# Feed-forward products in two column halves, in an attention and ReGLU kernel with a stored order

## The chip, the cores and the metric

The kernel runs on one core of a Trainium2 chip. The metric is the device time of one execution in microseconds. Before the change it was 398.09 us, the median of three runs (398.03, 398.09 and 399.47). A difference counts as faster or slower in this document when it exceeds 0.5% of that, about 2 us.

The core has a matrix engine (PE, with its weight loads shown apart as PEld), three engines for element work (DVE, ACT and POOL), and a queue of DMA issues that SyncE (SP) works off. Each engine takes its own instructions in the order in which the program lists them and waits at an instruction until what that one needs is there.

## The reference

Attention over 8 sequences of 576 rows with 8 heads of 64, each with 16 beacon rows in front that every query sees, and then a feed-forward layer over all 4608 rows:

```python
k_all = np.concatenate([beacon_k, k], axis=2)          # (8, 8, 592, 64)
v_all = np.concatenate([beacon_v, v], axis=2)
scores = scale * np.matmul(q, k_all.transpose(0, 1, 3, 2))
scores = np.where(causal, -1000000000.0, scores)       # the beacons are never masked
a = np.exp(scores - scores.max(-1, keepdims=True))
a /= a.sum(-1, keepdims=True) + 1e-09
attn_out = np.matmul(a, v_all)
x = attn_out.transpose(0, 2, 1, 3).reshape(4608, 512)
gate = np.maximum(x @ w_gate, 0.0)                      # 512 -> 1536
val = x @ w_val
out = gate * val @ w_out                                # 1536 -> 512
```

## The kernel before

**Attention.** A sequence is taken in two quads of two head pairs each. Score products (L828) use the array as four quarters of 64 rows by 64 columns; the last 16 query rows of all heads of a sequence go together through L878 with four strips of 32 columns. DVE adds the mask and takes the row's extreme (L776), ACT takes the exponential with the row's sum (L783), DVE the reciprocal (L789), and POOL multiplies with it (L794), which gives the tile `pb` (for the last rows `pa`). A transposing DMA on SP's queue (L914) turns `pb` into `pTb`, for the first sequence PE does it (L904). The value products (L924) then use the array as two halves of 128 rows by 64 columns, one head of the pair in each:

```python
def product(d0, w, c, last, rows, rhs):
    for hh in range(2):
        h = 2 * p + hh
        nc.tensor.matmul(ps.tile[64 * hh:64 * hh + 64, d0:d0 + w], t.v.tile[:rows, c, D * h:D * h + D],
                         rhs(64 * hh), start=(c == 0), stop=(c == last))
```

Their result goes from PSUM to `xT`, the transposed input of the feed-forward layer. Queries, keys and values come by DMA into staging tiles `st`, are rounded to bf16 tiles `h` (L546, L501, mostly on POOL) and turned (L557 and L630 on PE, L602 by DMA for the last sequence).

**Feed-forward.** The 4608 rows are cut into ten spans of 240 to 512 rows. For each of the twelve 128-column blocks of a span there is a `gate` task (L985) and a `val` task (L990), each of four matmuls with 128 by 128 weights over up to 512 columns, ACT takes the ReLU (L996), DVE multiplies (L1001) into `hT`. Twelve output products (L1016) for every 128 rows follow, in three `outp` tasks of four matmuls. All of these use the array whole, except the last 64 rows of all: there each matmul has 64 weight columns and the two halves of the array take the two halves of the output.

**Order.** Every piece is a task with an engine, and the text `ORDER` lists all tasks in the order in which they are written into the program. An entry is a task's number, a letter for the engine where there is a choice, and the tiles or PSUM banks it takes; `f4:7` is a filler, four matmuls on a zero tile (L1068), which stands where PE would otherwise idle. There are eight PSUM banks, and a product that takes a bank waits until the bank's former content is read. Since the order is fixed, an instruction at the head of an engine holds up all behind it.

I call a change from one way of dividing the array to another a switch of form. The forms are whole (L557, L904, L947, L985, L990, L1016, fillers), halves (L924), quarters (L828, L630) and strips (L878).

## Time and profile before

| | |
|---|---|
| Median of three runs | 398.09 us |
| Profiled execution | 397.86 us, span 396.1 us |
| PE busy | 382.1 us (96% of the span) |
| DVE, ACT, POOL busy | 280.1, 268.1, 231.4 us |
| Granted PE clock | 0.998 |

The span runs from the first to the last instruction; the rest of the profiled time lies around it. A busy PE is not a PE at its peak: a matmul row shows its whole passage, 379 ns for 512 columns, while the next one starts some 216 ns after it. What counts is therefore the distance between starts. In the views by line, "idle before" is the time the engine stood before an instruction and the name behind the arrow is what ended it; "issue" means that the profile shows nothing that it waited for. Attention ends near 333 us; after that PE does feed-forward products alone.

### The profile page before, as it was taken

What the parts mean: (1) busy time and instruction counts of PE and PEld (TensorE: products, weight loads), DVE (VectorE), ACT (ScalarE), POOL (GpSimd) and SP (SyncE); (2) the same over time, 40 slices, a digit from 0 to 9 for tenths busy, and PEclk for the clock granted to TensorE, in tenths of its full rate; (3) what the DMA queues carried; (4) which work ended last, traced back from release to release, by engine and by line L of the source; (5) the groups of instructions that cost most, each with busy time, mean ns of one, the idle gap of its engine ahead of it and who ended that gap; (6) DMA issues with size and microseconds to landing.
All of it is one profiled execution on the core that took longest, in us unless ns stands there. A gap on an engine that the chain in (4) does not pass through costs nothing.

```text
span 396.1 us, 10057 instructions
## 1 busy us (share of the span) xinstructions
PE 382.1 (96%) x3416; PEld 202.2 (51%) x3461; DVE 280.1 (71%) x1018; ACT 268.1 (68%) x832; POOL 231.4 (58%) x448
## 2 busy tenths in 40 slices
PE   6799999999999999999999999999999999999996
PEld 4568856654554445454444454544454544444443
DVE  5998899979967898878777885687847831431531
ACT  3999799897887787778775978587847723231121
POOL 3899779949695778495856766663891550000000
PEclk9999999999999999999999999999999999999999
DMA  7999999999999999989999899899889274000202
GB/s 188 231 228 225 212 223 214 206 214 214 242 187 224 268 205 201 202 225 169 223 208 229 181 211 191 182 191 185 153 165 201 52 130 117 26 0 2 107 29 93
DMA packets 184100, 68.89 MB, mean 174 GB/s; under 512 B 158384, under 2 KB 179504, under 8 KB 184048
## 3 DMA queue, kind: packets, MB, share of 16 engines
q1 hardware_dynamic: 179216, 63.46, 75.3%
q0 software_dynamic: 4752, 4.72, 7.3%
q8 instruction: 27, 0.44, 0.5%
q14 instruction: 25, 0.20, 0.2%
q10 hardware_dynamic: 80, 0.07, 0.1%
HBM read 38.54 MB, written 9.44 MB: 121 GB/s over the span
## 4 chain that ended last, share of the span: by engine, by line
PE 79%; DMA 7%; POOL 4%; DVE 3%; issue 3%; ACT 2%; SPq 1%; POOLq 0%; ACTq 0%; DVEq 0%
PE f L990 21%; PE f L985 21%; PE f L1016 20%; PE f L924 6%; PE f L828 5%; DMA pTb<-pb 4%; POOL pb L794 3%; PE f L557 2%; PE f L904 1%; POOL h L546 1%; DMA st<-in_q_dram 1%; ACT pb L783 1%; DVE f L776 1%; DMA st<-in_k_dram 1%; PE f L947 1%
## 5 line engine op out<-in xcount | busy, mean ns | idle before, releaser
L794 POOL TENSOR_SCALAR pb<-pb,small 128x256 bf16<-128x256 bf16 (+8 forms) x272 | 143.1, 546 | 53.8 <-DVE small L789 50.4
L783 ACT ACTIVATE pb<-f,small 128x320 bf16<-128x320 f32 (+8 forms) x272 | 144.3, 545 | 28.6 <-DVE small L776 19.3
L776 DVE CUSTOM_DVE_ANT_0 f<-f,mask 128x64 f32<-128x64 f32 (+8 forms) x288 | 136.2, 508 | 18.0 <-PE f L828 10.4
L985 PE MATMUL f<-xT,wg_r 128*128 128x512 bf16 (+3 forms) x468 | 107.7, 357 | 0.7
L990 PE MATMUL f<-xT,wv_r 128*128 128x512 bf16 (+3 forms) x464 | 106.0, 357 | 1.3 <-issue 0.5
L1001 DVE TENSOR_TENSOR hT<-g,f 128x512 bf16<-128x512 f32 (+3 forms) x120 | 73.8, 628 | 41.9 <-PE f L990 30.4
L1016 PE MATMUL f<-wo_r,hT 128*128 128x512 bf16 (+3 forms) x439 | 99.8, 374 | 1.7 <-issue 0.8
L996 ACT ACTIVATE g<-f 128x512 f32<-128x512 f32 (+3 forms) x120 | 65.1, 562 | 46.8 <-PE f L985 41.4
L990 PEld LDWEIGHTS <-wv_r 128*128 128x128 bf16 x480 | 44.6, 98 | 44.9 <-issue 3.5
L985 PEld LDWEIGHTS <-wg_r 128*128 128x128 bf16 x480 | 44.9, 98 | 43.7 <-issue 2.3
L1016 PEld LDWEIGHTS <-hT 128*128 128x128 bf16 (+3 forms) x456 | 42.0, 100 | 46.8 <-issue 2.3
L546 POOL TENSOR_SCALAR h<-st 128x512 bf16<-128x512 f32 (+1 forms) x88 | 47.8, 555 | 22.5 <-DMA st<-in_q_dram 4.9
L783 ACT ACTIVATION_READ_ACCUMULATOR pb<-f,small 128x1 f32 x272 | 58.1, 214 | 0.0
L776 DVE DVE_READ_ACCUMULATOR2_ANT small<- 128x1 f32 x296 | 41.5, 140 | 0.0
L828 PE MATMUL f<-kT,qT 64*64 64x64 bf16 (+7 forms) x640 | 34.0, 292 | 1.0 <-ACT kT L497 0.8
L499 DVE COPY osb<-f 128x512 f32<-128x512 f32 (+3 forms) x22 | 14.8, 674 | 22.6 <-PE f L1016 22.5
L497 ACT CAST xT<-f 128x240 bf16<-128x240 f32 (+2 forms) x39 | 14.9, 388 | 23.0 <-PE f L924 20.8
L924 PE MATMUL f<-pTb,v 128*64 128x320 bf16 (+3 forms) x488 | 27.3, 254 | 0.8 <-DMA pTb<-pb 0.7
L501 POOL TENSOR_SCALAR v<-st 128x512 bf16<-128x512 f32 (+1 forms) x38 | 23.6, 625 | 7.1 <-DMA st<-in_v_dram 6.9
L789 DVE RECIPROCAL small<-small 128x1 f32<-128x1 f32 (+3 forms) x136 | 19.8, 160 | 10.0 <-ACT pb L783 8.5
L924 PEld LDWEIGHTS <-v 128*64 128x64 bf16 (+1 forms) x512 | 21.3, 109 | 10.0 <-issue 5.7
L828 PEld LDWEIGHTS <-qT 64*64 64x64 bf16 x640 | 14.5, 105 | 22.5 <-issue 17.8
(64 smaller groups left out, 229.1 us busy)
## 6 DMA issues: line engine op xcount, KB each, us to landing
out_dram<-osb SPq DMA_DIRECT2D x34, 256.0 KB, 3.0
st<-in_k_dram SPq DMA_DIRECT2D x28, 256.0 KB, 4.5
st<-in_q_dram SPq DMA_DIRECT2D x28, 256.0 KB, 4.1
st<-in_v_dram SPq DMA_DIRECT2D x24, 256.0 KB, 4.9
st<-in_q_dram SPq DMA_DIRECT2D x16, 128.0 KB, 3.4
st<-in_k_dram SPq DMA_DIRECT2D x16, 128.0 KB, 3.1
st<-in_v_dram SPq DMA_DIRECT2D x8, 224.0 KB, 4.5
wv_r<-in_moe_w_val_dram POOLq DMA_DIRECT2D x3, 512.0 KB, 7.6
```

Source lines behind the costliest of these rows:

```text
L501: nc.gpsimd.tensor_scalar(dst, src, 1.0, 1.0, ALU.mult, ALU.mult)
L546: (nc.gpsimd if x.engine == "POOL" else nc.vector).tensor_scalar(to, src, by, 1.0, ALU.mult, ALU.mult)
L776: nc.vector.tensor_tensor_reduce(out=view(i, n - m), in0=view(i, n - m), in1=msk, scale=1.0, scalar=at(7) if m < n else 3.0e38, op0=ALU.ad ...
L783: nc.scalar.activation(ph.tile.rearrange("p a n -> p (a n)")[:, a:a + n], view(i), AF.Exp, bias=at(i), scale=-1.0, accum_out=at(4 + i))
L794: nc.gpsimd.tensor_scalar(one, one, at(8 + i), 1.0, ALU.mult, ALU.mult)
L828: nc.tensor.matmul(banks[k][b_].tile[64 * i:64 * i + 64, off:off + n], t.q.tile[r, 2 * g + i, 64 * j:64 * j + 64], t.kT.tile[r, 2 * g + i, ...
L924: nc.tensor.matmul(ps.tile[64 * hh:64 * hh + 64, d0:d0 + w], t.v.tile[:rows, c, D * h:D * h + D], rhs(64 * hh), start=(c == 0), stop=(c == ...
L985: nc.tensor.matmul(psg.tile[:, :mt], wg_r[:, ki, nf * P:(nf + 1) * P], xT[:, ki, m0:m0 + mt], start=(ki == 0), stop=(ki == KM - 1))
L990: nc.tensor.matmul(psv.tile[:, :mt], wv_r[:, ki, nf * P:(nf + 1) * P], xT[:, ki, m0:m0 + mt], start=(ki == 0), stop=(ki == KM - 1))
L996: r = add("ACT", c_act(mt), lambda _, psg=psg, g=g: nc.scalar.activation(g.tile[:, :mt], psg.tile[:, :mt], AF.Relu), (a,), (psg, g), -1000 ...
L1001: hid.append(add("DVE", c_dve(mt), lambda _, psv=psv, g=g, nf=nf: nc.vector.tensor_mul(hT[nf].tile[:, :mt], g.tile[:, :mt], psv.tile[:, :m ...
L1016: nc.tensor.matmul(ps[c].tile[64 * c:64 * c + rows, :w], hT[nf].tile[:, t0:t0 + rows], wo_r[:, nf, w * c:w * c + w], start=(nf == 0), stop ...
```

## The change

A task can be marked `w` in the stored order. A marked `gate`, `val` or `outp` task issues every matmul twice, for columns 0 to 63 and for columns 64 to 127 of its weights, each with its own weight load, into the upper and lower half of the same bank. This is the array form of the value products. The moving operand and the number of moving columns stay the same, so a pair does the work of one matmul. The order is a new one as well. The diff, cut to its core:

```diff
 ORDER = """
 ...
-394:0 1619 1620 1521 1613 2181 1601 1621 2174:3 1616 1565:0 1622 1627:6.7.4.5 403 1561:0 1623 1636 1563:2 1602 1562a 1628 1605 2182 400:2 1629 2185:0
 ...
+1621 1601 2174:3 1620 2181 1602 1612 1604 1619 1565:0 2176 1611 1622 1627:6.7.4.5 1561:0 1623 1563:2 1562v 2177w 1635 2185w:0 1636 1629 395 1638 2182w
 ...
@@ class Task
         self.start = None
+        self.narrow = False
@@ replay
-            t = self.tasks[int(what.rstrip("avg"))]
-            t.engine = engines.get(what[-1], t.engines[0])
+            t = self.tasks[int(what.rstrip("avgw"))]
+            t.engine, t.narrow = engines.get(what[-1], t.engines[0]), what[-1] == "w"
@@ kernel
+    def halves(x):
+
+        return ((0, 64), (64, 64)) if x.narrow else ((0, P),)
@@ ffn
-            def gate(_, nf=nf, psg=psg):
+            def gate(x, nf=nf, psg=psg):
                 for ki in range(KM):
-                    nc.tensor.matmul(psg.tile[:, :mt], wg_r[:, ki, nf * P:(nf + 1) * P], xT[:, ki, m0:m0 + mt],
-                                     start=(ki == 0), stop=(ki == KM - 1))
+                    for c, w in halves(x):
+                        nc.tensor.matmul(psg.tile[c:c + w, :mt], wg_r[:, ki, nf * P + c:nf * P + c + w], xT[:, ki, m0:m0 + mt],
+                                         start=(ki == 0), stop=(ki == KM - 1))
 ...
                     for nf in range(k * part, k * part + k):
-                        for c in range(halves):
+                        if groups == 1 and rows == P:
+                            for c, z in halves(x):
+                                nc.tensor.matmul(ps[0].tile[c:c + z, :w], hT[nf].tile[:, t0 + c:t0 + c + z],
+                                                 wo_r[:, nf, :w], start=(nf == 0), stop=(nf == NF - 1))
+                            continue
+                        for c in range(groups):
```

`val` is changed as `gate` is. The turning of rounded tiles (L557) could be marked too, but no such task is. Marked are 23 tasks: one `gate` of the first span (240 columns) and, from the fifth span on, 13 `outp`, 5 `gate` and 4 `val` tasks with 512 columns. With four matmuls each these are 92 pairs in place of 92 matmuls. The fillers shrink from 79 to 76 matmuls.

The new order is close to the old one. Of PE's 599 entries 109 stand elsewhere among their neighbours, mostly by one or two places. POOL and SP are reordered more, and five copies out of PSUM go from DVE to ACT.

The first place is PE's order at the value products of the seventh sequence's second quad, near 288 to 297 us. In the rows `v` and `hT` behind LDWEIGHTS are weights (values and hidden tiles), and the first number of a shape is the number of output rows. Before, the value products are followed by seven `outp` tasks, more value products, four feed-forward tasks and the strip scores:

```order
L924 MATMUL f<-pTb_80,v_87 64x64
L1016 LDWEIGHTS hT_106
L1016 MATMUL f<-wo_r,hT_106 128x512
...
L1016 MATMUL f<-wo_r,hT_121 128x512
L924 LDWEIGHTS v_87
L924 MATMUL f<-pTb_79,v_87 64x320
...
L924 MATMUL f<-pTb_79,v_87 64x128
L1016 LDWEIGHTS hT_106
L1016 MATMUL f<-wo_r,hT_106 128x512
...
L985 MATMUL f<-xT,wg_r 128x512
L878 LDWEIGHTS qT_84
```

After, with the same tasks but for one `outp` that has gone behind the second value products:

```order
L929 MATMUL f<-pTb_80,v_87 64x64
L1024 LDWEIGHTS hT_106
L1024 MATMUL f<-wo_r,hT_106 64x512
...
L1024 MATMUL f<-wo_r,hT_121 64x512
L929 LDWEIGHTS v_87
L929 MATMUL f<-pTb_79,v_87 64x320
...
L929 MATMUL f<-pTb_79,v_87 64x128
L1024 LDWEIGHTS hT_106
L1024 MATMUL f<-wo_r,hT_106 64x512
...
L991 MATMUL f<-xT,wg_r 64x512
L883 LDWEIGHTS qT_84
```

The form changed at four borders here (values to `outp`, `outp` to values, values to `outp`, `gate` to strips); now it changes at one, the last.

Counted along the whole of PE's order, the form changes 177 times before and 174 times after. In PE's first 50 entries, up to about 30 us of the trace before, the number rises from 24 to 27; behind them it falls from 153 to 147. The six fewer lie at four groups of marked tasks: one near 206 us, one near 254 us, three at the place shown, one near 308 to 313 us.

The second place is SP's queue near 257 to 272 us, in front of the transposition `pTb_80<-pb_74`, whose result the value products at 271.56 us read. Before:

```order
L914 DMA_TRANSPOSE pTb_81<-pb_73 128x25x128
L914 DMA_TRANSPOSE pTa_77<-pa_71 128x5x128
L588 DMA st_95<-in_k_dram 128x4x64 x2
L914 DMA_TRANSPOSE pTb_80<-pb_74 128x25x128
L602 DMA_TRANSPOSE qT_84<-h_101 128x4x128
```

After:

```order
L919 DMA_TRANSPOSE pTb_81<-pb_73 128x25x128
L1042 DMA out_dram<-osb_97 128x512
L919 DMA_TRANSPOSE pTb_80<-pb_74 128x25x128
L919 DMA_TRANSPOSE pTa_77<-pa_71 128x5x128
L607 DMA_TRANSPOSE kT_86<-h_100 128x4x128
```

The small transposition now stands behind it, the loads of `st_95` further ahead, and one store of the output has come between.

The third place is POOL's order there. The last two rows with `pb_74` are what that transposition waits for; `h` rows are rounded inputs, `v` rows rounded values. Before:

```order
L794 TENSOR_SCALAR pa_71<-pa_71,small 128x592
L794 TENSOR_SCALAR pb_74<-pb_74,small 128x384
L501 TENSOR_SCALAR v_88<-st_89 128x512
L794 TENSOR_SCALAR pb_74<-pb_74,small 128x448
L794 TENSOR_SCALAR pb_74<-pb_74,small 128x320
L546 TENSOR_SCALAR h_100<-st_91 128x512
L794 TENSOR_SCALAR pb_74<-pb_74,small 128x128
L794 TENSOR_SCALAR pb_74<-pb_74,small 128x576
L794 TENSOR_SCALAR pb_74<-pb_74,small 128x256
L546 TENSOR_SCALAR h_102<-st_92 128x512
```

After:

```order
L506 TENSOR_SCALAR v_88<-st_89 128x512
L799 TENSOR_SCALAR pb_73<-pb_73,small 128x384
L799 TENSOR_SCALAR pb_73<-pb_73,small 128x576
L799 TENSOR_SCALAR pb_74<-pb_74,small 128x128
L799 TENSOR_SCALAR pb_74<-pb_74,small 128x448
L799 TENSOR_SCALAR pa_71<-pa_71,small 128x592
L799 TENSOR_SCALAR pb_74<-pb_74,small 128x320
L551 TENSOR_SCALAR h_100<-st_91 128x512
L551 TENSOR_SCALAR h_102<-st_92 128x512
L799 TENSOR_SCALAR pb_74<-pb_74,small 128x576
L799 TENSOR_SCALAR pb_74<-pb_74,small 128x256
```

Three pieces of `pb_74` and the values' rounding have moved ahead of the row with `pa_71`, and the rounding of `st_92` has moved from behind the last two pieces to ahead of them. On DVE the reciprocal that these two need stands ahead of one feed-forward product (L1001) that it stood behind.

## The prediction

> I read the page first, then PE by stretches of time, PE's rows at the marked tasks, and last the engines behind the one long wait that PE has.

> **What bounds the kernel.** The page's span, its busy times and its slices:

> ```profile
> span 396.1 us, 10057 instructions
> PE 382.1 (96%) x3416; PEld 202.2 (51%) x3461; DVE 280.1 (71%) x1018; ACT 268.1 (68%) x832; POOL 231.4 (58%) x448
> PE   6799999999999999999999999999999999999996
> POOL 3899779949695778495856766663891550000000
> PEclk9999999999999999999999999999999999999999
> ```

> PE is busy in every slice, and its clock is never held back. By three stretches (microseconds from the start; length, PE busy, matmuls):

> ```profile
> 0.00:30.00 30.00, 24.23 (x260) 1.00 1.06 216
> 30.00:271.50 241.50, 237.82 (x2396) 1.00 1.01 209
> 271.50:392.30 120.80, 119.91 (x763) 1.00 0.44 95
> ```

> So after 30 us PE stands idle for 3.7 and 0.9 us, and the end moves with PE: with how long its matmuls take, how often the form changes, and with the few waits. That also caps the gain. The change removes no arithmetic.

> **The pair itself.** A marked task issues two half-width matmuls in place of one, so 92 pairs. The price of a pair against one whole matmul decides all else. The trace has the same form in the last 64 rows of the output and in the value products; here beside the whole form, PE's rows and then the loads:

> ```profile
> L1016 PE MATMUL f<-wo_r,hT 128*128 128x512 bf16 x391 | 92.3, 379 | 1.7 <-issue 0.8 <-ACT g L996 0.3
> L1016 PE MATMUL f<-wo_r,hT 128*64 128x256 bf16 x24 | 1.5, 275 | 0.0
> L1016 PEld LDWEIGHTS <-hT 128*128 128x128 bf16 x408 | 38.1, 98 | 44.9 <-issue 1.9
> L924 PEld LDWEIGHTS <-v 128*64 128x64 bf16 x448 | 18.1, 109 | 9.3 <-issue 5.7 <-DMA pTb<-pb 1.1
> L1016 PEld LDWEIGHTS <-hT 128*64 128x64 bf16 x24 | 1.2, 110 | 0.4 <-issue 0.4
> ```

> The 24 half matmuls are 12 pairs in 1.5 us. Less the last one's passage of 0.275 us, 11 distances of 0.11 us are left for 256 columns. Four whole matmuls of 512 columns take 1.03 us (rows of L985 below), which less 0.379 us leaves three distances of 0.217 us, twice that. So both halves stream at once, at full rate. Their loads are slow for their width, 110 ns for 64 columns against 98 ns for 128, but 24 of them fit in 1.2 us, one pair of loads in 0.1 us: the two run beside each other and under the matmuls. I cost the 92 pairs at nothing. [...] Upwards the bound is a pair whose two loads run in turn, 0.220 against 0.217 us, together +0.3 us. Below nothing there is no room, since the columns streamed are the same.

> [...]

> **Switches of form.** PE around the first place shown of the order (start, length, then the group):

> ```profile
> 287.74 0.88 PE L924 MATMUL f<-pTb,v 128*64 128x128 bf16 x16
> 288.55 6.22 PE L1016 MATMUL f<-wo_r,hT 128*128 128x512 bf16 x27
> 294.70 0.88 PE L924 MATMUL f<-pTb,v 128*64 128x320 bf16 x16
> 295.51 1.04 PE L1016 MATMUL f<-wo_r,hT 128*128 128x512 bf16 x4
> 296.39 1.03 PE L985 MATMUL f<-xT,wg_r 128*128 128x512 bf16 x4
> ```

> The seven `outp` tasks end at 294.77; their last matmul therefore starts at 294.77 - 0.379 = 294.39, and a next one of the same form would start at 294.61. The value products start at 294.70. A switch costs 0.09 to 0.10 us, and I take 0.10. Behind the first 30 us the order has six fewer (153 to 147): -0.6 us. Each is saved only if PE has its next work ready, so the bounds are -0.6 and 0. The three more in the first 30 us stand among fillers and waits (below), so I cost them at nothing, at most +0.3.

> **The wait at 271.56.** Two of the six lie ahead of this place, so I ask what they meet there. PE, then SP's queue, and the step of the chain of waits between them:

> ```profile
> 270.02 0.88 PE L924 MATMUL f<-pTb,v 128*64 128x320 bf16 x16
> 271.56 0.88 PE L924 MATMUL f<-pTb,v 128*64 128x128 bf16 x16 [0.66 <-DMA pTb<-pb]
> ```
> ```profile
> 257.23 4.21 SPq L914 DMA_TRANSPOSE pTb<-pb  x1
> 261.54 1.22 SPq L914 DMA_TRANSPOSE pTa<-pa  x1
> 262.81 1.12 SPq L588 DMA_DIRECT2D st<-in_k_dram  x2
> 264.03 4.28 SPq L914 DMA_TRANSPOSE pTb<-pb  x1
> ```
> ```profile
> 264.03 7.48 DMA pTb<-pb
> ```

> It is the one wait of PE after 30 us of more than a few tenths, and it ends when a transposition lands 7.48 us after its issue at 264.03. Whatever PE gains before it is lost unless this issue comes earlier. The queue is released of 1.22 + 1.12 us ahead of it and gets one store (some 0.5 us), so SP would be free near 262.0 instead of 263.9. The other condition is POOL and, ahead of it, DVE:

> ```profile
> 258.07 0.76 POOL L794 TENSOR_SCALAR pa<-pa,small 128x592 bf16<-128x592 bf16 x1 [2.50 <-DVE small L789]
> 261.06 0.62 POOL L546 TENSOR_SCALAR h<-st 128x512 bf16<-128x512 f32 x1
> 261.65 1.69 POOL L794 TENSOR_SCALAR pb<-pb,small 128x128 bf16<-128x128 bf16 x3
> 263.31 1.21 POOL L546 TENSOR_SCALAR h<-st 128x512 bf16<-128x512 f32 x2
> 261.28 0.69 DVE L1001 TENSOR_TENSOR hT<-g,f 128x512 bf16<-128x512 f32 x1 [0.17 <-ACT pb L783]
> 261.88 0.16 DVE L789 RECIPROCAL small<-small 128x2 f32<-128x2 f32 x1
> ```

> POOL idles 2.50 us at `pa`, while other rows behind it stand ready. The new order puts three `pb_74` rows and a value rounding in front of `pa`, and pays with one more rounding (0.6 us) ahead of the last two. The reciprocal for these two, at 261.88, now goes before a product of 0.69 us. So the two can start near 261.3 and end near 262.6, and the transposition issues some 1.4 us earlier, or 0.7 if the reciprocal stays late. PE gets there 0.2 us earlier, so 0.86 us are wanted. I take the wait as gone: -0.66; bounds -0.66 and, if nothing moves, +0.2 (the two switches eaten). The small transposition, pushed behind, is issued some 5 us later than now; its readers come after 273 us and it takes under 3 us (the row of all transpositions below has 2.6 as the least), so I cost it at nothing, with perhaps 1 us of cover left.

> **What else moves.** 109 PE entries, the five copies given to ACT, and many POOL and SP rows are reordered. In the trace before, PE had 3.7 + 0.9 us of idle time after 30 us, the wait just counted among it, so the new waits can cost more than the old ones can give back. I take +0.2 us; bounds -0.5 and +3 (next part). At the start:

> ```profile
> L1068 PE MATMUL f<-idle 128*128 128x256 bf16 x79 | 12.8, 302 | 2.3 <-DVE idle L442 2.0
> 12.52 1.16 PE L1068 MATMUL f<-idle 128*128 128x256 bf16 x9
> 14.85 0.62 PE L557 MATMUL f<-ident,h 128*128 128x128 bf16 x8 [1.17 <-DVE small L789]
> ```

> Fillers and waits for other engines fill this stretch. Three fillers less take nothing off the path, and a score group moved behind a turning fits in waits like that of 1.17 us; 0, with 0.5 us either way.

> **Sum.** 0 - 0.6 - 0.66 + 0.2 + 0 = -1.06 us. The profiled execution took 397.86 us and becomes 396.8; it lies 0.23 us under the median of the runs, so I give 397.0 us for the median. That is -0.3%, within the 0.5% which this measurement can tell from no change.

> **Rivals.** *The savings are eaten.* If the transposition lands at 271.5 as now, PE waits longer and only the four switches behind count: 398.09 - 0.4 = 397.7. For it: a reciprocal that depends on rows reordered on ACT and DVE. Against it: the freed SP queue.

> *POOL stalls in front of a transposition.* POOL takes its rows in order and stood 2.50 us at 258.07 and longer still here:

> ```profile
> 248.80 0.43 POOL L794 TENSOR_SCALAR pb<-pb,small 128x192 bf16<-128x192 bf16 x1 [3.14 <-DVE small L789]
> L914 SPq DMA_TRANSPOSE pTb<-pb x28: 3679/4188/5597, 63.1 to 323.4; - x28
> DMA to landing us min/median/max: 2.6/6.2/8.6
> ```

> The new order could put such a stall ahead of one of the 28 transpositions whose landing PE just meets, as at 271.56. PE then stands for the stall less what cover there is: 3.14 us on top of -0.6 gives 398.09 + 2.5 = 400.6. It decides the sign from 0.6 us on, and makes the kernel slower by over 0.5% from 2.6 us on. For it: most of POOL's rows moved. Against it: at the place I could follow, the move takes a stall away.

> *The start gives more.* If the first stretch loses 1 us of its waits, the forecast of 397.0 becomes 396.0. For it: 12.8 us of fillers and the waits among them. Against it: they end on DMAs and element work, which the marks don't touch.

> *The halves don't overlap.* A load of 110 ns shown by each of 92 pairs is +10.1 us, with the forecast 407. [...]

> **Chances.** Forecast 0.43 (396.2 to 397.6), eaten 0.20, POOL's stall 0.25, a better start 0.09, no overlap 0.03. Under 396.1 lie the better start and the lower edge of the forecast, 0.12. Over 400.1 lie 0.17 of the stall, the last rival and a little for several small new waits, 0.21. The rest, 0.67, is within 0.5%. The range 395.8 to 400.6 leaves out the last rival and the ends of the second and third.

> **What would show it.** PE's rows with half the columns: 512-column pairs 0.217 us apart. At 288 to 297 us one group of half form with no load idling in it. The value products near 271 us without a wait for the DMA, their transposition issued near 262.6 us. PE's busy share unchanged. The forecast is wrong if pairs lie further apart, or if a wait of over 1 us for a transposition or for PSUM appears on PE.

## The result and the profile after

| | before | after |
|---|---|---|
| Median, first series (20 runs each) | 398.71 us | 397.46 us |
| Ratio, 95% interval | | 0.9965 (0.9949 to 0.9981) |
| Median, second series (28 and 12 runs) | 398.32 us | 397.80 us |
| Ratio, 95% interval | | 0.9975 (0.9956 to 0.9994) |
| Profiled execution, span | 397.86, 396.1 us | 398.12, 396.4 us |

The changed kernel is 0.25 to 0.35% faster. That is less than the 0.5% taken as a difference, but both intervals lie below 1. The forecast was 397.0 us. One of the 20 runs of the changed kernel took 557.51 us at a clock of 0.66, and one of the 23 runs of the kernel before in the first series of experiments 1356.71 us at full clock; the ratios leave both out.

The page of the profile after, and PE by the three stretches used before (length, PE busy, matmuls, granted clock, DMA share, GB/s):

```profile
span 396.4 us, 10292 instructions
PE 386.1 (97%) x3550; PEld 205.3 (52%) x3550; DVE 279.2 (70%) x1013; ACT 269.2 (68%) x837; POOL 232.3 (59%) x448
PEclk9899999999999999999999999999999999999999
```
```profile
0.00:30.00 30.00, 24.37 (x245) 0.94 1.05 199
30.00:271.50 241.50, 240.52 (x2439) 1.00 1.00 211
271.50:392.30 120.80, 120.80 (x868) 1.00 0.42 97
```

Three things stand out. This execution is longer than the profiled one of before although the median is lower. The clock was not full in the first 30 us. And PE seems to have gained 3.6 us of busy time behind 30 us, far more than the forecast takes off. Most of the last one is an artefact. The page of before counts 3416 matmuls beside 3461 weight loads; this page counts 3550 of both. Where the record of a matmul is missing, the trace shows idle time that was none: 0.05 us for one out of a stream of 512 columns (two distances of 0.216 us less one passage of 0.379 us), up to 0.16 us elsewhere.

PE after at the two places of the prediction (start, length, group):

```profile
271.37 0.55 PE L833 MATMUL f<-kT,qT 64*64 64x512 bf16 x12
271.85 1.57 PE L929 MATMUL f<-pTb,v 128*64 128x320 bf16 x32
...
288.73 0.88 PE L929 MATMUL f<-pTb,v 128*64 128x128 bf16 x16
289.44 5.35 PE L1024 MATMUL f<-wo_r,hT 128*64 128x512 bf16 x48
294.62 0.86 PE L929 MATMUL f<-pTb,v 128*64 128x320 bf16 x16
295.31 1.89 PE L1024 MATMUL f<-wo_r,hT 128*64 128x512 bf16 x16
297.04 1.03 PE L991 MATMUL f<-xT,wg_r 128*64 128x512 bf16 x8
```

The value products run as one group of 32 without a wait. At 289 to 298 us the half form goes through: eight matmuls of `gate`, four pairs, take 1.03 us, as four whole ones did. The six `outp` tasks end at 294.79, their last pair started at 294.79 - 0.379 = 294.41, and the value products follow 0.21 us behind it, the distance within a form.

**Where the time went.** The tasks are the same in both kernels, so I took the start of a task's first weight load in each trace and subtracted that of before. Only tasks are shown that stand at comparable places in both orders. Positive is later, in us; the heads are the times in the trace of before. The rows below the first two are the experiments of the next section.

| kernel | 26.2 | 37.2 | 62.6 | 101.8 | 270.0 | 271.6 | 287.7 | 299.1 | 316.4 | 390.9 |
|---|---|---|---|---|---|---|---|---|---|---|
| after | 1.53 | 1.63 | 2.42 | 2.38 | 1.83 | 0.96 | 0.99 | 0.65 | 0.40 | 0.28 |
| after, second profile | 1.49 | 1.58 | 1.67 | 1.63 | 1.07 | 0.20 | 0.22 | -0.11 | -0.37 | -0.49 |
| new order, no marks | 0.47 | 0.57 | 0.82 | 0.78 | 0.48 | -0.40 | -0.37 | -0.37 | -0.53 | -0.65 |
| old order, marks | 0.65 | 0.64 | 0.64 | 0.67 | 1.53 | 0.66 | 0.69 | 0.36 | 0.25 | 0.24 |
| old order, queue freed | 1.42 | 1.42 | 1.42 | 1.42 | 1.62 | 0.93 | 0.93 | 0.93 | 0.93 | 0.93 |
| new start, old rest | 0.84 | 0.94 | 1.04 | 1.18 | 1.21 | 0.98 | 0.98 | 0.98 | 0.98 | 0.67 |
| old start, new rest | 1.57 | 1.57 | 1.57 | 1.39 | 0.83 | -0.04 | -0.01 | -0.34 | -0.61 | -0.73 |
| the same, second profile | -0.14 | -0.14 | -0.14 | -0.32 | -0.88 | -1.76 | -1.73 | -2.06 | -2.33 | -2.45 |

The changed kernel loses 1.5 us at the start and regains 2.15 us behind 62.6 us, alike in both of its profiles: 0.6 up to the wait near 271.6 us, 0.87 there and some 0.7 behind it. At 57.8 us its first profile alone has a wait of 0.57 us for a weight's DMA.

Part of the loss at the start belongs to no kernel. PE by windows of 3 us, of before and then of the changed kernel (behind the comma PE busy, matmuls, granted clock, DMA share, GB/s):

```profile
15.00:18.00 3.00, 2.49 (x32) 1.00 1.24 175
18.00:21.00 3.00, 2.84 (x38) 1.00 1.25 216
```
```profile
15.00:18.00 3.00, 2.09 (x22) 0.89 1.21 181
18.00:21.00 3.00, 3.00 (x28) 0.54 1.24 218
```

In the changed kernel the clock was halved for one stretch of 3.4 us, from 17.3 to 20.7 us. The last section shows that this happened to every one of these kernels that was measured more than once, in some executions and not in others. The rows of the table at 26.2 us with 1.4 us or more have such a stretch in the 16 to 21 us of their trace; the one of 0.65 (old order, marks) has it at 10 to 14 us. The rows of 0.47, 0.84 and -0.14 have none.

### The profile page after: what moved, and what is told of

The parts are those of the page before. It is cut to its first block, busy times and chain, and to the rows that moved or that the text cites. A ratio compares the mean times of both kernels' runs of the same rounds, so it can differ in the third digit from the quotient of the medians.

```text
span 396.4 us, 10292 instructions
## 1 busy us (share of the span) xinstructions
PE 386.1 (97%) x3550; PEld 205.3 (52%) x3550; DVE 279.2 (70%) x1013; ACT 269.2 (68%) x837; POOL 232.3 (59%) x448
## 4 chain that ended last, share of the span: by engine, by line
PE 91%; DMA 4%; DVE 1%; ACT 1%; SPq 1%; issue 0%; POOL 0%; DVEq 0%; ACTq 0%
PE f L991 24%; PE f L997 23%; PE f L1024 22%; PE f L833 7%; PE f L929 6%; PE f L562 2%; DMA wo_r<-in_moe_w_out_dram 2%; PE f L909 2%; DMA st<-in_q_dram 1%; PE f L1028 1%; PE f L952 1%; PE f L883 1%; PE f L1080 1%; DMA st<-in_beacon_k_dram 1%; PE f L635 1%; ACT pb L788 1%
## 5 line engine op out<-in xcount | busy, mean ns | idle before, releaser
L799 POOL TENSOR_SCALAR pb<-pb,small 128x448 bf16<-128x448 bf16 (+8 forms) x272 | 142.9, 541 | 59.0 <-DVE small L794 57.9
L781 DVE CUSTOM_DVE_ANT_0 f<-f,mask 128x576 f32<-128x576 f32 (+8 forms) x288 | 136.1, 510 | 20.7 <-PE f L833 10.0
L991 PE MATMUL f<-xT,wg_r 128*128 128x512 bf16 (+5 forms) x504 | 108.6, 358 | 0.2 <-DVE kT L504 0.2
L997 PE MATMUL f<-xT,wv_r 128*128 128x512 bf16 (+4 forms) x496 | 108.1, 359 | 0.1
L1003 ACT ACTIVATE g<-f 128x512 f32<-128x512 f32 (+3 forms) x120 | 66.0, 561 | 45.7 <-PE f L991 38.9
L1024 PE MATMUL f<-wo_r,hT 128*128 128x512 bf16 (+1 forms) x460 | 94.9, 379 | 0.6 <-DMA wo_r<-in_moe_w_out_dram 0.6
L991 PEld LDWEIGHTS <-wg_r 128*128 128x128 bf16 (+1 forms) x504 | 45.2, 99 | 44.8 <-issue 3.1
L997 PEld LDWEIGHTS <-wv_r 128*128 128x128 bf16 (+1 forms) x496 | 45.2, 98 | 44.5 <-issue 2.4
L1024 PEld LDWEIGHTS <-hT 128*128 128x128 bf16 (+1 forms) x460 | 38.7, 100 | 43.5 <-issue 2.6
L504 DVE COPY osb<-f 128x512 f32<-128x512 f32 (+3 forms) x22 | 14.8, 673 | 20.7 <-PE f L1024 12.0
L794 DVE RECIPROCAL small<-small 128x2 f32<-128x2 f32 (+3 forms) x136 | 20.4, 161 | 9.7 <-ACT pb L788 8.7
L502 ACT CAST xT<-f 128x240 bf16<-128x240 f32 (+2 forms) x42 | 15.4, 375 | 12.4 <-PE f L929 10.0
```

What stands on the lines that cost most here:

```text
L781: nc.vector.tensor_tensor_reduce(out=view(i, n - m), in0=view(i, n - m), in1=msk, scale=1.0, scalar=at(7) if m < n else 3.0e38, op0=ALU.ad ...
L799: nc.gpsimd.tensor_scalar(one, one, at(8 + i), 1.0, ALU.mult, ALU.mult)
L991: nc.tensor.matmul(psg.tile[c:c + w, :mt], wg_r[:, ki, nf * P + c:nf * P + c + w], xT[:, ki, m0:m0 + mt], start=(ki == 0), stop=(ki == KM ...
L997: nc.tensor.matmul(psv.tile[c:c + w, :mt], wv_r[:, ki, nf * P + c:nf * P + c + w], xT[:, ki, m0:m0 + mt], start=(ki == 0), stop=(ki == KM ...
L1003: r = add("ACT", c_act(mt), lambda _, psg=psg, g=g: nc.scalar.activation(g.tile[:, :mt], psg.tile[:, :mt], AF.Relu), (a,), (psg, g), -1000 ...
L1024: nc.tensor.matmul(ps[0].tile[c:c + z, :w], hT[nf].tile[:, t0 + c:t0 + c + z], wo_r[:, nf, :w], start=(nf == 0), stop=(nf == NF - 1))
```

## The experiments

**The marks and the order apart.** First the new order with no task marked, and the order before with 22 of the 23 marks (all but the `gate` of the first span).

```diff
-... 1562v 2177w 1635 2185w:0 1636 1629 395 1638 2182w ...
+... 1562v 2177 1635 2185:0 1636 1629 395 1638 2182 ...
```

> The new order with no task marked. In this order the form then changes 182 times instead of 174. My theory: the wait near 271.6 us stays away, since it went with the order of SP, POOL and DVE; eight switches at 0.10 us come back, so it is 0.8 us slower than the changed kernel, a ratio of about 0.9985 to the kernel before. Rival (the marks carry the gain): a ratio of 1.000 or more. Rival (marks are worth nothing, the order all): 0.9965.

> The old order with 22 of the 23 marks (all but the one in the first span): the same groups of tasks as in the changed kernel, in the form of the value products beside them. Six switches fewer than before, 171 against 177, and nothing else moved. My theory: two of the six lie ahead of the wait near 271.6 us and are eaten by it, so that the wait grows from 0.82 to about 1.0 us, and four count: -0.4 us, a ratio of 0.999 to the kernel before. Rival (the marks carry the whole gain): a ratio near 0.9965, -1.4 us. Rival (marks cost): over 1.000.

Without marks: 398.19 us, ratio 1.0005 (0.9973 to 1.0037). Marks in the old order: 398.15 us, ratio 0.9987 (0.9961 to 1.0013). Neither interval leaves 1 out, so the medians alone tell only that neither part is worth much over 0.4%; the first interval leaves out 0.9965, the rival by which the order has the whole gain, the second leaves out none of its cases. The traces tell more. From 271.6 us to the end the new order gains 0.25 us without marks (-0.40 to -0.65) and 0.68 with them, 0.43 more for four switches. The marks in the old order gain 0.42 there (0.66 to 0.24). Both give 0.11 us for each (counted along PE's order, there are four fewer changes of form behind this place in both pairs).

The second kernel also did what neither the theory nor a rival had: the wait at 271.56 was gone, though SP's order was as before. SP's queue and PE there:

```profile
264.89 4.45 SPq L919 DMA_TRANSPOSE pTb<-pb  x1
271.55 1.57 PE L929 MATMUL f<-pTb,v 128*64 128x320 bf16 x32
```

PE came 1.53 us late to this place, the issue only 0.86 us, and the transposition landed 5.9 us behind its issue in place of 7.5. The landing of one and the same transposition lies between 5.6 and 7.7 us over the eight traces that I compared. So the wait comes and goes with the execution. In its place PE stood 0.60 us for a small transposition near 173 us, which had been issued 5.7 us earlier, and 0.30 us for another near 221 us. POOL's rows came late with PE (the last for this transposition ended at 264.87 us, 263.34 before), but SP's queue hardly did: it was free at 264.28 us (263.93 before), and here POOL alone let the transposition go.

**What held up the transposition.** In the old kernel only the two entries of SP's order that stood ahead of it are moved behind it.

```diff
-... 389:1 2132:1 2133:5 1448 2130:8 1518 1576:0 1470 ...
+... 389:1 2132:1 2133:5 1448 2130:8 1518 1470 ...
-... 2139:1 390:6 1449 ... 2137:0 1516 1492:1 1525 ...
+... 2139:1 1449 ... 2137:0 1516 1492:1 1576:0 390:6 1525 ...
```

> The kernel before, with two entries of SP's order (the small transposition pTa and the load of st, 1.22 and 1.12 us on the queue) moved directly behind the transposition pTb_80 that stood at 264.03 us; nothing else changes. Theory (the queue and POOL's rows together held the issue back): with the queue free, POOL's norms, which end at 263.34, are the only condition left, the issue comes at about 263.4, the wait of 0.66 us on PE shrinks to 0.0 to 0.2 us, and all PE work behind it is about 0.6 us earlier. Rival 1 (POOL alone set the issue): issue and wait stay as they were within 0.15 us. Rival 2 (the landing is set by how busy the DMA engines are): the issue comes earlier but the landing stays near 271.5.

PE is 1.62 us late here, so 263.4 becomes 265.0. The issue came at 264.99, and PE's wait is gone but for 0.16 us (the group of 32 takes 1.73 us, 1.57 without a wait):

```profile
264.99 3.80 SPq L914 DMA_TRANSPOSE pTb<-pb  x1
268.84 1.30 SPq L914 DMA_TRANSPOSE pTa<-pa  x1
```
```profile
271.64 1.73 PE L924 MATMUL f<-pTb,v 128*64 128x320 bf16 x32
```

The landing took 7.46 us as before, so no shorter transfer explains it. The queue was worth 0.69 us (1.62 to 0.93), and everything behind stays 0.69 us ahead to the end. Of the 0.87 us that the new order gains at this place, these are 0.69. For the rest, with a landing that long, the issue has to come earlier than POOL's old rows allow. It does in the changed kernel:

```profile
264.35 4.41 SPq L919 DMA_TRANSPOSE pTb<-pb  x1
```

In PE's own time that is 264.35 - 1.83 = 262.52 us, against 264.03 before and 264.99 - 1.62 = 263.37 us here. Its landing also took only 6.3 us.

This trace has all its records and the old order, so it also shows what PE's idle time was before. By the stretches of the prediction:

```profile
30.00:271.50 241.50, 240.99 (x2425) 1.00 1.02 208
271.50:392.30 120.80, 120.65 (x788) 1.00 0.45 99
```

That is 0.51 and 0.15 us, and with the 0.69 us that the edit took away about 1.35 us, in place of the 4.6 us that the prediction read out of its trace.

**Many more pairs, and many more switches.** Two kernels mark tasks of the last 60 us, where PE does feed-forward work alone: all 70, or every second one.

```diff
-2343:2 2330 2319v:2 2345:3 2320 2344:0 2262 2351:7 2346:11 2355:2 2353:0 2356:0 2348:1 2349:5
+2343w:2 2330 2319v:2 2345w:3 2320 2344:0 2262 2351w:7 2346:11 2355w:2 2353w:0 2356:0 2348:1 2349w:5
```

In the second kernel the line reads:

```diff
+2343:2 2330 2319v:2 2345w:3 2320 2344:0 2262 2351:7 2346:11 2355w:2 2353:0 2356:0 2348:1 2349w:5
```

> The changed kernel with all 70 whole feed-forward tasks behind the last value products marked too: 280 more matmuls become pairs, and the form changes twice less. My theory (a pair costs what a whole matmul costs): the stretch from the last value products to the end is as long as in the changed kernel, within 0.3 us, and pairs stand 0.216 to 0.217 us apart. Rival (the two weight loads of a pair run in turn, 0.220 us): +1 us over the stretch. Rival (a load shows in each pair): +30 us.

> The changed kernel with every second of the 70 whole feed-forward tasks behind the last value products marked: 35 tasks become pairs and the form changes 68 times more, where PE has nothing else to wait for. My theory (0.10 us for a switch, nothing for a pair): +6.6 to +6.8 us on the stretch behind the last value products. Rival (a switch between whole and half form is cheaper when weights can be loaded ahead, and the 0.10 us read from the trace are the wait for the value products' data): under +3 us.

All marked: 398.95 us in the one execution, which had two half-clock stretches at its start. PE is 1.34 us late at 316.4 and 0.81 at 390.9, a gain of 0.53 us where the changed kernel gains 0.12, so 280 more pairs took nothing. (Of the 0.41 us between them 0.2 are two switches and 0.2 an earlier weight load at the last task, which the matmuls do not follow.) The clearest rows are the output products at the end, 36 matmuls whole (the changed kernel), then 36 pairs:

```profile
383.35 7.93 PE L1024 MATMUL f<-wo_r,hT 128*128 128x512 bf16 x36
391.21 1.50 PE L1028 MATMUL f<-wo_r,hT 128*64 128x256 bf16 x24
```
```profile
384.19 7.94 PE L1025 MATMUL f<-wo_r,hT 128*64 128x512 bf16 x72
391.96 1.48 PE L1029 MATMUL f<-wo_r,hT 128*64 128x256 bf16 x24
```

7.93 and 7.94 us. The last change of form shows too: 391.21 - 383.35 = 7.86 us from the first output product to the last form, against 7.77 where there is none.

Every second marked: 406.32 us, and PE's delay grows from 0.87 to 8.27 us where in the changed kernel it fell by 0.12. The order has 68 switches more: 7.52 / 68 = 0.11 us for each. A piece of it (the row with x12 holds one whole and one halved task):

```profile
357.05 1.91 PE L991 MATMUL f<-xT,wg_r 128*128 128x448 bf16 x12
358.89 1.04 PE L997 MATMUL f<-xT,wv_r 128*128 128x512 bf16 x4
359.86 0.95 PE L991 MATMUL f<-xT,wg_r 128*64 128x448 bf16 x8
360.74 0.93 PE L997 MATMUL f<-xT,wv_r 128*128 128x448 bf16 x4
```

From 358.89 to 359.86 are 0.97 us; four matmuls of 512 columns without a switch need 0.86.

**The start and the rest apart.** Up to about 87 us the one order, behind it the other. The first of these two has the old start with its fillers and the new rest with 22 marks, the second the reverse with one mark.

```diff
 ORDER = """
-6 4 22:0 2 9 10 ...
-... 164:5 772a 810 160:1
+10 1 22:0 9 12 26:1 ...
+... 772a 795 810 160:1
 830 812 835:7.4 ...
```

> The order before up to about 87 us, fillers included, and behind that the new order with its marks (22 of 23). Theory (the new order loses about 1.1 us in the first 50 us, of which 0.5 at 47 to 49 us, and gains behind 270 us): the PE work at 50 to 270 us is on time with the kernel before or up to 0.3 us ahead, the wait at 271.56 is gone, the end is 1.3 to 1.6 us earlier than before with an equal clock, about 396.4 us and 0.996 of the time before, 1 us faster than the changed kernel. Rival (the late part gains only because it starts late, since work that starts earlier waits for the same landings): PE waits again near 271 us and the end is within 0.3 us of the changed kernel's.

> The new order up to about 87 us (one marked task), and behind that the order before without marks. Theory: PE is 1.0 to 1.2 us late from 50 to 270 us at an equal clock, the wait at 271.56 takes up about 0.7 us of it, and the end is 0.3 to 0.5 us later than before. Rival (the wait's landing comes later by the same amount, since all its suppliers are late too): the end is 1.0 to 1.2 us later than before, about 399.2 us.

> The changed kernel once more, unaltered, beside the three that follow. Expected: about 397.4 us, as in its first measurement, ratio to before 0.996 to 0.998.

> The order before up to about 87 us and the new one behind it, once more. Theory (the new start costs 0.6 to 1.1 us at an equal clock): 0.6 to 1.0 us faster than the changed kernel in the same series, about 396.5 us. Rival (the difference of the first measurement, 396.60 against 397.46 in another series, was the difference of the series): within 0.3 us of the changed kernel.

Old start, new rest: 396.60 us, ratio 0.9952 (0.9933 to 0.9971); in the series beside the changed kernel 396.21 against 397.80 us, 0.9944 (0.9923 to 0.9965) against 0.9975. New start, old rest: 398.97 us, ratio 1.0011 (0.9984 to 1.0038). The second interval has 1 in it; that the new start costs rests on the hybrid, which is faster than both kernels, by 1.6 us than the changed one in the one series. Executions with a mean clock of 0.998 or more give the same there: 397.99 us in the median before (20), 397.49 changed (6), 395.94 hybrid (8). At the same half-clock stretch in the trace (1.57 and 1.49 us at 26.2) it is 0.24 us ahead of the second profile of the changed kernel, and its trace at full clock ends 2.45 us ahead of before. By the traces its start is worth 0.24 us with such a stretch and 0.6 to 1.0 us without; why the medians show more is open.

The reverse kernel took little from the wait: 1.21 us late ahead of it, 0.98 behind it. The issue was 0.79 us late too, and PE still stood 0.43 us. The theory had 0.7 taken up; the rival nothing. The end, 0.67 us late in the trace, lies between the two as well.

What is lost at the start begins with one load. It brings the queries that DVE, PE and POOL all need near 14 us, and in these five traces it is the longest step of the chain of waits there. Of before, the changed kernel, its second profile, the hybrid and the new order without marks:

```profile
9.51 4.74 DMA st<-in_q_dram
```
```profile
9.14 5.74 DMA st<-in_q_dram
```
```profile
9.26 5.60 DMA st<-in_q_dram
```
```profile
9.21 4.85 DMA st<-in_q_dram
```
```profile
9.58 4.89 DMA st<-in_q_dram
```

It lands at 14.06 to 14.46 us in six of the seven traces with the old start (15.31 in the seventh) and at 14.47 to 15.34 us in the seven with the new one, from issues between 9.1 and 9.9 us in all of them. In the four traces that have neither a half-clock stretch nor the longer filler of below, the delay at 26.2 us follows it: -0.18 us at the landing gives -0.14 (hybrid), 0 gives 0 (before), 0.23 gives 0.47 (no marks), 0.83 gives 0.84 (new start, old rest). Why the transfer takes longer was not tested, nor whether the new order is the cause. The rest is where the first sequence's probabilities are turned on PE, in the hybrid and then in the order without marks:

```profile
21.97 0.43 PE L833 MATMUL f<-kT,qT 64*64 64x512 bf16 x4
22.38 0.84 PE L909 MATMUL f<-ident,xT 128*128 128x128 bf16 x12
```
```profile
22.07 0.43 PE L833 MATMUL f<-kT,qT 64*64 64x512 bf16 x4
23.02 0.49 PE L909 MATMUL f<-ident,xT 128*128 128x128 bf16 x6 [0.51 <-POOL xT L799]
```

With three fillers less PE is back on time at 22 us, but POOL, whose rows hang on the same load, is not, and PE stands for it. The wait of 0.40 to 0.52 us is in all seven traces of the new start; of the old one, two show 0.29.

**The clock at the start.** Two kernels lengthen one filler near 14 us from 9 to 20 matmuls, where PE stands: in the changed kernel, as shown, and at the same place in the hybrid.

```diff
-... 469:2.4 460 f9:7 425 451 ...
+... 469:2.4 460 f20:7 425 451 ...
```

> The changed kernel with one filler near 14 us lengthened from 9 to 20 matmuls, so that PE does not idle from 13.7 to 15.4 us. Theory (the half-clock windows of 3.4 us in the first 22 us, about 1.1 us of delay each, come from PE idling just there): the windows go in most executions, and the median falls by 0.4 to 0.6 us below that of the changed kernel. Rival 1 (they come from other idle stretches or from chance): the same share of executions has them and the median is unchanged within 0.3 us. Rival 2 (the longer filler itself delays PE): the start is later by up to 1 us.

> The hybrid with the filler near 14 us lengthened from 9 to 20 matmuls. Theory (PE idling there brings the half-clock windows): almost no execution with a mean granted clock under 0.998, against 4 of 12 in the hybrid, and a median 0.3 to 0.5 us lower, about 396.1 us. Rival (the windows come from elsewhere, or the filler is in the way): the same share of such executions, median within 0.2 us or up to 0.5 us higher.

396.85 us, ratio 0.996 (0.9945 to 0.9975), and 396.33 us, ratio 0.994 (0.9919 to 0.9962). Two of 12 and two of 8 executions had a mean clock under 0.998, where the changed kernel had 8 of 19 and 6 of 12 and the hybrid 4 of 12 twice. That speaks for the theory, weakly; 4 of 20 against 22 of 55 could be chance. In neither trace does a stretch follow the lengthened place; the first has one ahead of it, at 10.1 to 13.5 us. The filler may also be in the way: the hybrid's trace with it, at full clock, is 0.65 us later at 26.2 us than without it (0.51 against -0.14), but its load landed 0.33 us later, which accounts for half of that. In the hybrid no gain is left: 396.33 against 396.21. Against the changed kernel the 396.85 was measured in another series, so its 0.6 us stays open.

**The tail in halves, on the hybrid.**

> The hybrid with the last 70 feed-forward tasks in halves too, 280 more pairs and two switches fewer (the rows at the very end are in halves in any case). Theory (pairs cost nothing, a switch 0.1 us): 0.2 us faster than the hybrid, about 396.4 us. Rival (a pair costs something that was too small to see in 92): 280 pairs with even 5 ns each would make it 1.2 us slower than the hybrid.

396.12 us, ratio 0.9943 (0.992 to 0.9966), 0.09 us under the hybrid. The trace has 0.4 us at the last task's first load, of which 0.2 is the load itself, which here starts 0.21 us ahead of its matmuls (390.66 against 390.87 us) and in the hybrid with them (388.49 us); the matmuls give the two switches. It is the fastest version that ran, by a margin that the medians don't resolve.

## Why the prediction was right, and where not

The predicted time, 397.0 us, was 0.5 us under the first median and 0.8 under the second, which lies 0.2 us above the band of the likeliest case. As a gain on the kernel before, 1.06 us were forecast, and the two series measured 1.25 and 0.52 us. By its steps:

- *Pairs at nothing.* Right. 36 pairs took 7.94 us and 36 whole matmuls 7.93. Had each of the 280 pairs of the marked tail shown a load of 110 ns, that would be 31 us, and nothing was seen. Four whole matmuls do not show theirs, of 98 ns each, either: they take 1.03 us.
- *Six switches behind 30 us at 0.10.* Right: 0.11 us from 68 added ones, 0.11 from the four behind 271 us.
- *The wait at 271.56.* Right in the mechanism: SP's queue held the issue 0.69 us past POOL's rows, and POOL's rows come earlier too. The issue was forecast near 262.6 and came at 262.5 in PE's time. The term was 0.66 and measured 0.87 us: the 0.66 us run from the end of the last passage, but without a wait the next matmul starts 0.2 us before that end (the group of 32 took 1.57 us, two groups of 16 took 0.88 us each). Its size belongs to the execution, though. In the three traces with SP's old order PE stood 0.66, 0.43 and 0 us there.
- *What else moves, +0.2 with -0.5 and +3 as bounds.* Wrong in sign. Without marks the new order gains 0.34 us from 62.6 us to the wait and 0.25 behind it, 0.6 in all, in small pieces that I did not follow to single rows. (The five copies given to ACT are a balance: 16 tasks go from DVE to ACT and 13 the other way.) What the term rested on was wrong as well: 4.6 us of idle time where about 1.35 were true, and the sign of the missing records, 391 matmuls beside 408 loads of one line, stood in the prediction's own rows.
- *The start at 0 with 0.5 either way.* Wrong, the step that failed. The new start costs 0.6 to 1.0 us in the traces at full clock (0.47 and 0.84 at 26.2 us against -0.14 of the hybrid). The prediction took the fillers for cover that the moved work could use. But the chain there goes over a load, DVE and POOL, which the fillers don't lengthen and their removal doesn't shorten; the load landed later, for a reason that stays open, and PE waited for POOL 0.5 us further on.

Behind 62.6 us both profiles of the changed kernel gain 2.15 us where the steps had 1.06: 0.2 more at the wait, 0.1 more at the switches, 0.8 at what else moves. The start takes 0.6 to 1.0 of it back. So the total was right to 0.5 us with two terms off by some 0.8 us in opposite directions; that they cancel is luck.

Of the rivals, the savings were not eaten, the start gave nothing but took, the halves overlap, and no transposition on the queue came late. A stall of POOL in front of a turning did come, at 23 us and on PE, and was under the 0.6 us from which it would have decided. The range of 395.8 to 400.6 was wider upwards than the result needed.

## What to carry to other kernels

Splitting a whole matmul into two column halves cost nothing here with 512 streaming columns (36 pairs took 7.94 us, 36 whole matmuls 7.93) or with 448 (0.92 us for four pairs in the marked tail as for four whole matmuls), and every change of form that it saved was worth 0.11 us of PE. When an order is rewritten, follow the loads and the engines that feed PE through the start, where fillers stand: they hide that PE is not what sets the pace there, and half a microsecond lost at one load cost as much as four or five switches gave. Before idle time is read from a trace, compare the counts of matmuls and weight loads.

## What was not expected of the hardware

PE's granted clock fell to 0.5 for one or two stretches of 3.4 us within the first 22 us in some executions and not in others. By the mean clock this happened to every kernel measured more than once: 8 of 28 executions of the kernel before in the last series had a mean clock under 0.998. Those took 399.71 us in the median, the other 20 took 397.99; for the hybrid it was 397.19 (4) against 395.94 us (8). In the two kernels of the marked tail the profiled execution had two such stretches. PE by windows of 3 us, of the one with all tasks marked, which is the changed kernel at this place:

```profile
15.00:18.00 3.00, 1.91 (x15) 0.53 1.16 165
18.00:21.00 3.00, 3.00 (x26) 0.50 1.24 222
21.00:24.00 3.00, 3.00 (x34) 0.83 1.22 197
```

One stretch made the order before 1.1 us later (1.42 in the queue experiment, less the 0.34 that PE was late ahead of it). No stretch followed 3.4 us without work: the longest that PE stood behind its first 2 us was 2.5 us (every second task marked). PE waited 1.27 to 2.48 us near 14 us in the seven traces with a half-clock stretch behind that place, and 0.96, 1.17, 1.35 and 1.88 us in four without, so the length of the wait alone does not decide it.
